# Attention decode on one core: the whole loads of values issued by ScalarE instead of SyncE

## The chip, the cores and the metric

The kernel runs on one core of a Trainium2 chip. A core has five instruction streams that run on their own and wait for each other by semaphores: TensorE (PE in the profile; its weight loads are PEld), VectorE (DVE), ScalarE (ACT), GpSimd (POOL) and SyncE (SP). Transfers between HBM and the on-chip memory are issued by an instruction on one of these streams and are then carried out by 16 DMA engines that the core's queues have in common. The metric is device time in microseconds: the median of several runs. Before the change it is 1301.58 us (three runs, 1301.52 to 1301.68).

## The reference

One token for each of B = 2 sequences is decoded through attention with a cache and then through a gated feed-forward block. D = 448, H = 16 heads of 256, 8192 cached positions, F = 1792, all in float32:

```
q = (layernorm(x) @ wq)                    # 2 x 16 heads x 256
p = softmax(q . k_cache / 16)              # 2 x 16 x 8192
o = p . v_cache                            # 2 x 16 x 256
h = x + o @ wo
n = layernorm(h)
out = h + ((n @ w_gate) * (n @ w_up)) @ w_down
```

Each of the 32 pairs of head and sequence has its own keys and its own values of 8192 x 256 floats, 8 MB each. So 512 MB of caches are read once, and next to them some 24 MB of weights. Nearly all of the work is reading.

## The kernel before

A pair of head and sequence is called a query here, numbered 0 to 31. Its keys lie in 128 partitions, 64 rows of 256 floats in each, so a whole load is 128 rows of 64 KB.

**Stages of a query i.** `load_k(i)` brings its keys. `scores(i, part)` multiplies them with q and sums over 256 on VectorE, first a part of 16 rows for each partition (4096 elements), then one of 48 (12288 elements). `top(i)` takes the maximum of each partition on VectorE; TensorE turns it over into `sm`. `softmax(i)` finishes the maximum (`nm`, VectorE), spreads it (TensorE, then `nb` on ScalarE), takes the exponentials into `p` (ScalarE) and sums them (TensorE); `norm(i)` takes the reciprocal `rl` on VectorE. `load_v(i)` brings the values. `mix(i)` multiplies `p` with them on TensorE into `o_ps`. `mixed(i)` copies the result out (`o_sb`, ScalarE), brings it into columns (TensorE into `sm`) and scales it by `rl` (`oT`, ScalarE); after every second query TensorE adds it through `wo` to `acc_ps`. After queries 1, 5, 9, ..., 25 `queries` computes the next q of two heads on TensorE, and ScalarE copies them into `q`.

**Buffers.** The keys have room for 112 of such rows in each partition (`k_sb`), one whole load and three quarters of another: the keys of query n+1 may be written when VectorE is done with the first part of query n. The values have room for one whole load (`v_sb`): the values of query n may be written when TensorE has mixed those of n-1.

**Order of the work.** The main loop over n (0 to 32) writes, on each engine, the work of several queries: scores of n, softmax of n-1 between the two steps of the first part, mix of n-1 at the end. In it the loads are written in this order: `load_v(n-1)` at its start, `load_k(n+1)` after the first part of the scores of n, and at n = 1, 9, 17, 25 a load of weights (`load_w`, 3.5 MB, the last one 2.6 MB). All of them are issued by SyncE, one after the other; each waits for its buffer there. The class `Orders` derives the waits from what each instruction reads and writes. Queries 0 to 27 (`i < LOOP`, with LOOP = EARLY = 28) are run by TensorE in a loop, and their loads of values count up one semaphore, `e_v`, that this loop takes. Values of queries 28 to 31 come in two or three pieces (the table `LATE`), some of them into room that the keys no longer need. Behind them come the weights of the feed-forward block, in the keys' room.

TensorE works in the order of the queries: for query i it turns the maximum over, spreads it, sums the exponentials, mixes, brings the result into columns and, where it is due, computes new q; only then does it turn over the maximum of query i+1. VectorE needs that last result (`nm`) between the two steps of the first part of query i+2.

```
        if n > 0:
            load_v(n - 1, parts[0])
        if n < NQ:
            scores(n, 0, (lambda: softmax(n - 1)) if n > 0 else None)
        ...
        if n + 1 < NQ:
            load_k(n + 1)
```

Of the kernel before, what the change touches and what calls it, by code (L numbers as in the profile page):

```python
# [68 lines left out]
LOOP = EARLY  # L69
# [146 lines left out]
def decode_block(nc, x, k_cache, v_cache, w, wg, wu, wd, out):  # L216
# [31 lines left out]
    buffers = {"k": k_sb, "v": v_sb}  # L248
# [17 lines left out]
    def keys(cache, i, lo, hi):  # L266
        h, b = divmod(i, B)
        return cache[b, h].rearrange("(p j) d -> p j d", p=P)[:, lo:hi, :]

    def load_keys(name, cache, i, lo, hi, buf, at, event=None):  # L270
        o.load(
            "SP", name, buffers[buf][:, at : at + hi - lo, :], keys(cache, i, lo, hi),
            writes=[(buf, at * DH, (at + hi - lo) * DH)], event=event,
        )

# [3 lines left out]
    def load_k(i, lo=0, hi=NJ):  # L279
        load_keys(f"d_k_{i}_{lo}", k_cache, i, lo, hi, "k", k_base(i) + lo)  # L280
# [8 lines left out]

    def load_v(i, part):  # L290
        lo, hi, buf, at = part
        load_keys(f"d_v_{i}_{lo}", v_cache, i, lo, hi, buf, at, "e_v" if i < LOOP else None)

    def load_w(name, k, lo, hi, event=None):
        o.load("SP", name, w_sb[:, lo:hi], w[k][:, lo:hi], writes=[("w", lo, hi)], event=event)
# [90 lines left out]
    def q_at(h):  # L386
        return h % 2 * (1 + h // 2 % 2)

    for k in range(2):
        for b in range(B):  # L390
            for c in range(DC):
                at = c * 2 * DH + (k * DH if c < DC - 1 else 0)
# [5 lines left out]
            at = q_at(k)  # L398
# [213 lines left out]
    for n in range(NQ + 1):  # L612
        hp, at = divmod(n, 2 * B)
        parts = v_parts(n - 1) if n > 0 else []
        if n > 0:
            load_v(n - 1, parts[0])
# [10 lines left out]
        for part in parts[1:]:  # L627
            load_v(n - 1, part)
# [37 lines left out]
    at = 0  # L666
# [191 lines left out]
```

## Time and profile before

| what | value |
|---|---|
| median of the runs | 1301.58 us (1301.52 to 1301.68) |
| span of the profiled execution, first to last instruction | 1300.5 us |
| VectorE busy | 1130.8 us (87%) |
| TensorE busy | 488.8 us (38%) |
| ScalarE busy | 62.6 us (5%) |
| read from HBM | 561.19 MB, 432 GB/s over the span |
| SyncE's queue, packets | 12096, 561.30 MB |
| ScalarE's queue, packets | 4 (the token's own 3.5 KB) |

Times in the views are in microseconds from the start of the span. In a timeline a row is a start, a duration, the engine, the line of the kernel and the operation as output<-input. Rows of SPq and ACTq are the instructions that issue a transfer on SyncE's and ScalarE's queue. All instructions are recorded by one helper, so that their line is L229 (L176 for transfers) and the names of the tiles tell them apart. In the chain of waits each row is a start, a duration and what the time went to; a row DMA begins with the issue of a transfer and ends with its landing.

### The profile page before, as it was taken

The numbers are of one execution on the slowest core, as the hardware profiler recorded it, in microseconds if no ns is written. First come the engines' busy times: TensorE is split into PE (matmuls) and PEld (weight loads), VectorE is DVE, ScalarE is ACT, GpSimd is POOL, SyncE is SP. The second block draws the span as 40 slices with busy tenths as digits, with TensorE's granted clock in tenths as the row PEclk, the third lists the DMA queues.
The fourth block names the chain that finished last, engine by engine and source line by source line (L and its number), as shares of the span: only waits on it lengthen the run. The fifth ranks groups of instructions, "written<-read, shape, count | busy, mean of one in ns | idle before, by whom it ended". The sixth has DMA issues, their size and how long they took to land.

```text
span 1300.5 us, 6955 instructions
## 1 busy us (share of the span) xinstructions
PE 488.8 (38%) x2972; PEld 168.9 (13%) x2972; DVE 1130.8 (87%) x275; ACT 62.6 (5%) x184; POOL 1.4 (0%) x9
## 2 busy tenths in 40 slices
PE   3035422363331633215343063432424334243368
PEld 2011100120100201002101021010111001010113
DVE  7996988888988689888889868898888897889991
ACT  1000000000000000000000000000000000000000
POOL 0000000000000000000000000000000000000000
PEclk8566756686656766558666576665766667666578
DMA  9999999999999999999999999999999999999998
GB/s 414 423 434 448 424 437 431 427 441 423 448 424 435 448 423 443 427 439 429 435 435 423 433 448 423 448 424 443 427 443 427 423 436 445 426 438 429 435 433 374
DMA packets 12111, 561.45 MB, mean 432 GB/s; under 512 B 1602, under 2 KB 1732, under 8 KB 1988
## 3 DMA queue, kind: packets, MB, share of 16 engines
q1 hardware_dynamic: 12096, 561.30, 99.8%
q8 instruction: 6, 0.10, 0.0%
q14 instruction: 5, 0.04, 0.0%
q10 hardware_dynamic: 4, 0.00, 0.0%
HBM read 561.19 MB, written 0.11 MB: 432 GB/s over the span
## 4 chain that ended last, share of the span: by engine, by line
DMA 70%; DVE 29%; PE 0%; issue 0%; SPq 0%
DMA k_sb<-in_A_k_cache_dram 68%; DVE k_sb L229 14%; DVE s L229 14%; DMA k_sb<-in_wd_dram 2%; DVE nm L229 0%; PE y_ps L229 0%; SPq L176 0%; DVE m L229 0%; PE sm L229 0%; DVE v_sb L229 0%; DVE rl L229 0%
## 5 line engine op out<-in xcount | busy, mean ns | idle before, releaser
L229 DVE TENSOR_TENSOR k_sb<-k_sb,q 128x12288 f32<-128x12288 f32 (+2 forms) x67 | 549.6, 8203 | 130.3 <-DMA k_sb<-in_A_k_cache_dram 130.3
L229 DVE TENSOR_REDUCE s<-k_sb 128x48 f32<-128x12288 f32 (+2 forms) x67 | 549.3, 8198 | 0.2
L229 PE MATMUL o_ps<-v_sb,p 128*2 128x512 f32 x2000 | 288.2, 739 | 397.7 <-PEq L183 387.6
L229 PEld LDWEIGHTS o_ps<-v_sb,p 128*2 128x2 f32 x2000 | 53.7, 97 | 603.8 <-issue 591.3
L229 PE MATMUL sm<-nm,ones 1*128 1x1 f32 x64 | 16.6, 326 | 191.7 <-PEq L183 175.1
L229 PE MATMUL sm<-ident,m 128*1 128x128 f32 x32 | 10.9, 341 | 137.0 <-PEq L183 106.1
L229 PE MATMUL q_ps<-w_sb,xb 128*128 128x256 f32 (+1 forms) x172 | 59.3, 503 | 0.0
L229 ACT ACTIVATE o_sb<-o_ps 128x512 f32<-128x512 f32 x32 | 19.1, 597 | 703.9 <-PE o_ps L229 703.9
L229 PE MATMUL sm<-sel,o_sb 128*128 128x1 f32 x256 | 33.7, 253 | 25.8 <-PEq L183 22.9
L229 PE MATMUL acc_ps<-w_sb,oT 128*2 128x448 f32 x60 | 36.6, 749 | 15.9 <-PEq L183 11.0
L229 PEld LDWEIGHTS sm<-nm,ones 1*128 1x128 f32 x64 | 14.6, 283 | 201.2 <-issue 183.5
L229 PEld LDWEIGHTS sm<-sel,o_sb 128*128 128x128 f32 x256 | 31.8, 195 | 55.6 <-issue 48.2
L229 PEld LDWEIGHTS q_ps<-w_sb,xb 128*128 128x128 f32 x172 | 33.7, 200 | 30.0 <-issue 27.6
L229 PE MATMUL sm<-lsum,ones 128*128 128x1 f32 x64 | 17.5, 342 | 26.0 <-PEq L183 23.1
L229 ACT ACTIVATE nb<-sm 128x1 f32<-128x1 f32 x32 | 5.5, 171 | 395.7 <-PE sm L229 395.7
L229 PEld LDWEIGHTS sm<-ident,m 128*1 128x1 f32 x32 | 2.6, 81 | 149.8 <-issue 115.3
L229 PEld LDWEIGHTS sm<-lsum,ones 128*128 128x128 f32 x64 | 15.6, 303 | 28.0 <-issue 24.7
L229 ACT ACTIVATE q<-q_ps,rstd 128x512 f32<-128x512 f32 (+1 forms) x18 | 11.5, 640 | 71.9 <-PE q_ps L229 71.9
L229 PE MATMUL o_ps<-k_sb,p 128*2 128x512 f32 x48 | 9.3, 934 | 6.1 <-DMA k_sb<-in_A_v_cache_dram 6.1
L229 ACT ACTIVATE p<-s,nb 128x64 f32<-128x64 f32 x32 | 11.1, 347 | 1.0
L229 DVE TENSOR_TENSOR v_sb<-k_sb,q 128x6144 f32<-128x6144 f32 x1 | 6.6, 6557 | 4.8 <-DMA k_sb<-in_A_k_cache_dram 4.8
L229 PE MATMUL q_ps<-k_sb,xr 128*32 128x256 f32 (+3 forms) x96 | 10.0, 506 | 1.6 <-DMA k_sb<-in_B_w_gate_dram 1.6
(79 smaller groups left out, 85.1 us busy)
## 6 DMA issues: line engine op xcount, KB each, us to landing
v_sb<-in_A_v_cache_dram SPq DMA_DIRECT2D x4, 4096.0 KB, 30.5
w_sb<-in_w_dram SPq DMA_DIRECT2D x3, 3584.0 KB, 37.8
v_sb<-in_A_v_cache_dram SPq DMA_DIRECT2D x1, 6144.0 KB, 24.3
k_sb<-in_A_k_cache_dram SPq DMA_DIRECT2D x1, 5120.0 KB, 24.6
v_sb<-in_A_v_cache_dram SPq DMA_DIRECT2D x2, 2048.0 KB, 27.3
k_sb<-in_A_v_cache_dram SPq DMA_DIRECT2D x1, 4096.0 KB, 35.3
k_sb<-in_B_w_gate_dram SPq DMA_DIRECT2D x1, 3136.0 KB, 32.4
k_sb<-in_A_k_cache_dram SPq DMA_DIRECT2D x1, 3072.0 KB, 11.6
```

Of the source, the lines that this page charges most:

```text
L229: o.put(engine, lambda: f(*args, **kw), r, w, mark, event)
```

## The change

The loads of values of queries 0 to 27 are issued by ScalarE instead of SyncE. Nothing else is changed: the same transfers into the same buffers, at the same place of the main loop, with the same semaphore.

```diff
-    def load_keys(name, cache, i, lo, hi, buf, at, event=None):
+    def load_keys(name, cache, i, lo, hi, buf, at, event=None, by="SP"):
         o.load(
-            "SP", name, buffers[buf][:, at : at + hi - lo, :], keys(cache, i, lo, hi),
+            by, name, buffers[buf][:, at : at + hi - lo, :], keys(cache, i, lo, hi),
             writes=[(buf, at * DH, (at + hi - lo) * DH)], event=event,
         )
...
-        load_keys(f"d_v_{i}_{lo}", v_cache, i, lo, hi, buf, at, "e_v" if i < LOOP else None)
+        load_keys(
+            f"d_v_{i}_{lo}", v_cache, i, lo, hi, buf, at, "e_v" if i < LOOP else None,
+            by="ACT" if i < LOOP else "SP",
+        )
```

On SyncE, around the first load of weights in the loop, the order before is:

```order
L176 DMA k_sb<-in_A_k_cache_dram 128x16384
L176 DMA v_sb<-in_A_v_cache_dram 128x16384
L176 DMA k_sb<-in_A_k_cache_dram 128x16384
L176 DMA w_sb<-in_w_dram 128x7168
L176 DMA v_sb<-in_A_v_cache_dram 128x16384
L176 DMA k_sb<-in_A_k_cache_dram 128x16384
L176 DMA v_sb<-in_A_v_cache_dram 128x16384
```

and after the change, from the first part of the first keys on:

```order
L176 DMA k_sb<-in_A_k_cache_dram 128x6144
L176 DMA k_sb<-in_A_k_cache_dram 128x10240
L176 DMA k_sb<-in_A_k_cache_dram 128x16384 x2
L176 DMA w_sb<-in_w_dram 128x7168
L176 DMA k_sb<-in_A_k_cache_dram 128x16384 x8
L176 DMA w_sb<-in_w_dram 128x7168
```

Keys and values no longer alternate there; eight loads of keys follow one another between two loads of weights.

On ScalarE, from the end of query 1 (the first query after which new q are computed) to the exponentials of query 3, the order before is:

```order
L229 ACTIVATE o_sb<-o_ps 128x512
L229 ACTIVATE oT<-sm,rl 128x2
L229 ACTIVATE q<-q_ps,rstd 128x2x256 x2
L229 ACTIVATE nb<-sm 128x1
L229 ACTIVATE p,lsum<-s,nb 128x64
L229 ACTIVATE o_sb<-o_ps 128x512
L229 ACTIVATE oT<-sm,rl 128x2
L229 ACTIVATE nb<-sm 128x1
L229 ACTIVATE p,lsum<-s,nb 128x64
```

and after the change:

```order
L229 ACTIVATE o_sb<-o_ps 128x512
L229 ACTIVATE oT<-sm,rl 128x2
L229 ACTIVATE q<-q_ps,rstd 128x2x256 x2
L176 DMA v_sb<-in_A_v_cache_dram 128x16384
L229 ACTIVATE nb<-sm 128x1
L229 ACTIVATE p,lsum<-s,nb 128x64
L229 ACTIVATE o_sb<-o_ps 128x512
L229 ACTIVATE oT<-sm,rl 128x2
L176 DMA v_sb<-in_A_v_cache_dram 128x16384
L229 ACTIVATE nb<-sm 128x1
L229 ACTIVATE p,lsum<-s,nb 128x64
```

The first of the two loads brings the values of query 2, the second those of query 3. A load now stands behind `oT` of the query before it and, after every fourth query, behind the two copies into `q` as well; on SyncE it waited for the end of the mix alone.

## The prediction

> **What bounds the kernel now.** I read the page first: its engines, the DMA slices and the queues.
>
> ```profile
> PE 488.8 (38%) x2972; PEld 168.9 (13%) x2972; DVE 1130.8 (87%) x275; ACT 62.6 (5%) x184; POOL 1.4 (0%) x9
> DMA  9999999999999999999999999999999999999998
> GB/s 414 423 434 448 424 437 431 427 441 423 448 424 435 448 423 443 427 439 429 435 435 423 433 448 423 448 424 443 427 443 427 423 436 445 426 438 429 435 433 374
> q1 hardware_dynamic: 12096, 561.30, 99.8%
> q10 hardware_dynamic: 4, 0.00, 0.0%
> ```
>
> No engine is full; the DMA engines are, in every slice but the last. A table of stretches (busy times, clock, DMA share, GB/s) says the same of single queries, and the chain of waits shows how a query's keys pass:
>
> ```profile
> 208.80:247.40 38.60, 12.12 (x77) 3.83 (x77) 35.01 (x7) 1.47 (x5) 0.00 (x0) 0.59 1.00 435
> 247.40:286.00 38.60, 18.20 (x95) 6.85 (x96) 35.01 (x7) 2.16 (x6) 0.00 (x0) 0.69 1.00 435
> 93.13 38.10 DMA k_sb<-in_A_k_cache_dram
> 140.22 29.89 DMA k_sb<-in_A_k_cache_dram
> 170.14 4.43 DVE k_sb L229
> 174.56 0.19 DVE nm L229
> 174.75 4.34 DVE s L229
> 179.11 29.67 DMA k_sb<-in_A_k_cache_dram
> 217.76 29.66 DMA k_sb<-in_A_k_cache_dram
> ```
>
> Keys are issued every 38.65 us (179.11 to 217.76); in that time one load of keys and one of values pass, so a load takes 19.33 us. A load of keys is on its way for 29.67 us: the first 10.3 it stands behind values. So SyncE's queue always holds 10 us of work when the next load joins it. VectorE, at 35.0 of 38.6 us, waits for keys. Only more bytes a second or fewer idle DMA moments could shorten this stage, and the DMA share is 1.00: what matters is whether the change keeps the engines fed.
>
> **The change, part by part.**
>
> *Issue.* 28 issues move. SyncE's cost 0.33 us; ScalarE's one issue before cost 0.53:
>
> ```profile
> 159.94 0.33 SPq L176 DMA_DIRECT2D v_sb<-in_A_v_cache_dram  x1
> 0.73 0.53 ACTq L176 DMA_DIRECT2D v_sb<-in_A_x_dram  x1
> 175.49 0.17 ACT L229 ACTIVATE nb<-sm 128x1 f32<-128x1 f32 x1 [13.48 <-PE sm L229]
> ```
>
> That is 15 us spread over an engine busy for 62.6; behind the load stands `nb`, which waits 13.48 us for TensorE anyway. I cost the issues at nothing; without that cover they would be 15 us.
>
> *When values are issued.* Timeline of an ordinary query (2) and of one with new q (5):
>
> ```profile
> 150.80 9.07 PE L229 MATMUL o_ps<-v_sb,p 128*2 128x512 f32 x64 [13.26 <-PEq L183]
> 161.75 0.26 ACT L229 ACTIVATE oT<-sm,rl 128x2 f32<-128x2 f32 x1 [1.21 <-PE sm L229]
> 266.87 9.06 PE L229 MATMUL o_ps<-v_sb,p 128*2 128x512 f32 x64 [12.73 <-PEq L183]
> 287.57 0.27 PE L229 MATMUL sm<-ident,m 128*1 128x128 f32 x1
> 287.77 0.69 ACT L229 ACTIVATE q<-q_ps,rstd 128x512 f32<-128x512 f32 x1 [2.75 <-PE q_ps L229]
> ```
>
> TensorE starts when values land. SyncE issued the next ones 9.1 us later (159.94). ScalarE must first finish `oT`, 11.2 us after landing (162.01), or in seven turns (after queries 1, 5, ..., 25) the second `q`, 21.6 us after (288.46).
>
> *Two queues instead of one.* Before, keys in flight kept the DMA busy while values were mixed, because loads passed in order of issue. With two queues nothing orders keys against values; q10's 4 packets show no sharing, so it is bounded from both sides: each engine finishes one load's share first (first rival), or the queues alternate. I take alternating: q1's 12096 packets are its 84 transfers times 144, 128 rows and 16 small ones each, so the unit an engine handles is a row of 64 KB, an eighth of its share, 2.42 us.
>
> *What alternating does.* Keys need 9.0 us from landing to next issue (170.12 to 179.11), values 11.2, so values fall back 2.2 us a query until two ties hold. First, both are then in flight together and land nearly together, and while both buffers are being used up nothing is in flight. Second, keys cannot run ahead: `nm` needs TensorE's turn of the maximum, which stands behind the previous query's mix and `oT`. From values landing: 11.2, about 0.5 to the turn, 0.3 for it, `nm` 0.2, reduction 4.34, 0.1 to the issue: keys are issued at 16.6, 5.4 us behind values.
>
> Start latency (issue to landing less own transfer time) is bounded by two issues into an idle DMA:
>
> ```profile
> w_sb<-in_w_dram SPq DMA_DIRECT2D x1, 896.0 KB, 4.8
> out_dram<-v_sb SPq DMA_DIRECT2D x1, 56.0 KB, 1.6
> ```
>
> 4.8 - 2.1 = 2.7 and 1.6 - 0.1 = 1.5; I take 2.0. Then, with even sharing: values have the DMA alone for 5.4 us; the other 13.93 take twice as long; they land 33.25 after their start, keys 5.4 later, and the next values start after 11.2 + 2.0: a query takes 46.45 us, 7.8 of them idle. A turn with new q takes 33.25 + 21.6 + 2.0 = 56.85. Keys by their own path would start at 38.65 + 9.0 + 2.0 = 49.65, before 46.45 + 5.4, so the tie holds, and it restores itself: keys further behind gain 2.2 us a query.
>
> *Start and end.*
>
> ```profile
> 26.07 0.33 SPq L176 DMA_DIRECT2D v_sb<-in_A_v_cache_dram  x1
> 56.95 12.94 DVE L229 TENSOR_TENSOR k_sb<-k_sb,q 128x12288 f32<-128x12288 f32 x1
> 57.05 0.33 SPq L176 DMA_DIRECT2D k_sb<-in_A_k_cache_dram  x1
> 64.97 9.31 PE L229 MATMUL o_ps<-v_sb,p 128*2 128x512 f32 x64 [10.20 <-PEq L183]
> 69.81 0.15 DVE L229 RECIPROCAL rl<-sm 128x1 f32<-128x1 f32 x1
> 1140.22 9.29 PE L229 MATMUL o_ps<-v_sb,p 128*2 128x512 f32 x64 [12.73 <-PEq L183]
> 1149.58 0.33 SPq L176 DMA_DIRECT2D v_sb<-in_A_v_cache_dram  x1
> 1159.42 4.43 DVE L229 TENSOR_TENSOR k_sb<-k_sb,q 128x4096 f32<-128x4096 f32 x1 [3.58 <-DMA k_sb<-in_A_k_cache_dram]
> 1296.47 2.03 PE L229 MATMUL y_ps<-k_sb,v_sb 128*32 128x112 f32 x64 [0.71 <-DMA k_sb<-in_wd_dram]
> ```
>
> Values 0 (issued 26.07) now share with keys 1, and what was through at 64.97 still is: both land there, keys about 2 us sooner, at 63. Keys 2 are issued 9.0 later, at 72 (57.05 before), and start at 74: 9 us idle. Values 1 wait for `oT` 0, whose `rl` (69.81) follows the long multiplication (56.95): issue 72 + 12.9 + 0.6 = 85.5, start 87.5. By halves (13.4 us of keys 2 done alone, then keys 2, the weights of 8.44 = 38.10 - 29.66, and keys 3 beside them) they land at 126.2 and values 2 start at 149.8. From there to the start of values 27 are 19 ordinary turns and 6 with new q: 882.6 + 341.1, so 1373.5; landing 1406.7; SyncE's first late values start at 1406.7 + 9.2 + 2.0 = 1417.9. From keys 29 landing (1159.4) to the last landing (1296.4) the DMA ran without a gap for 137.0 us, then 4.1 to the end. Sum: 1417.9 + 137.0 + 4.1 = 1559. The three other loads of weights fall into the idle 7.8 us and add at most 1 each.
>
> Row by row instead of evenly, values send three whole rows (7.25 us) before keys get a turn, and land at 7.25 + 5 x 4.83 = 31.4, 1.85 sooner; over 25 turns 46 us less: 1513. Rows are the unit, but sixteen engines need not turn in step and the slowest sets the landing; I take the middle, 1536, and add the 1.1 us by which the median of the runs exceeds the span: **1537 us**, 18% slower. Latency of 1.5 or 2.7 moves it by -13 or +18: own range 1490 to 1590.
>
> **Rivals.**
>
> *An engine finishes a load's share (eight rows) before it turns to the other queue.* The order is then that of before. A turn with new q leaves 21.6 + 2.0 - 19.33 = 4.3 us empty, unless weights (8.44) lie behind the keys, as in four of the seven; 3 x 4.3 = 13, so 1314 (1313 to 1317). Elsewhere the 10.3 us of work ahead cover the 2.1 us of delay. The same time follows if both queues feed one. For it: each engine's eight rows come from one instruction. Against it: rows are packets of their own in the counts. The Trainium skill, "DMA: Bandwidth & Descriptors", section "Queues, rings and completion order", says that a DMA engine goes round its queues packet by packet and that a packet is typically 9 to 17 descriptors; eight rows and an end would be one packet by that, and the time this rival's. No run shows yet which it is here.
>
> *Turns of several rows.* With four, values land after 12 rows, 29.0 us instead of 33.25: 25 x 4.25 = 106 less than 1559, 1453.
>
> *Not slower: order as in the first rival, and a second queue raises the rate,* one queue's rows filling the gaps between the other's. The 13 us are made up from 561.3 MB / (1293 - 14) = 439 GB/s on; at the slices' highest, 448, transfers take 1253 instead of 1293: 1314 - 40 = 1274. For it: slices of 448. Against: stretches cut at landings give 435 at a share of 1.00, so the 448 look like bytes booked at a row's end. With alternating rows no such rate could repay 235 us.
>
> **How the numbers follow.** Alternating 0.64, 1537; whole shares 0.20, 1314; coarse turns 0.07, 1453; not slower 0.09, of it 0.04 faster. About 0.2% (2.6 us) is what a measurement here can tell from no change; by it: faster 0.04, same 0.05, slower 0.91. The range takes in the second case and nearly all of the first: 1308 to 1595; the likeliest's own is 1490 to 1590.
>
> **What would show it.** Right: q10 with about 4036 packets and 235 MB; DMA slices at 8, some 365 GB/s; values and keys landing 33 to 39 us after issue, keys some 5 us behind; `nm` waiting for TensorE's `sm`; idle DMA after each landing, most after new q; VectorE busy as before but 74% of the span. Wrong: keys landing about 29.7 us after issue as now, which is the first rival, or a rate above 435 in stretches where both queues hold work. The forecast falls if queues do not alternate, and its size if keys are issued well before `oT`.

## The result, and the profile after

The changed kernel takes 1545.64 us (median of five runs, 1541.89 to 1546.97) against 1301.52 us (1301.33 to 1301.68) before: a ratio of 1.1871, 95% interval 1.1858 to 1.1883. The profiled execution spans 1544.3 us.

Lines of its page: engines, DMA slices, the two hardware queues and a group of instructions. The last two are from the list of transfers: how often keys and whole loads of values were issued, and the median us from issue to landing.

```profile
PE 480.4 (31%) x2972; PEld 164.2 (11%) x2972; DVE 1133.4 (73%) x275; ACT 62.6 (4%) x184; POOL 1.4 (0%) x9
DMA  9799889957899579886799958988589895988998
q1 hardware_dynamic: 8064, 326.42, 49.0%
q10 hardware_dynamic: 4036, 234.89, 36.1%
L229 DVE TENSOR_REDUCE nm<-sm 1x1 f32<-1x128 f32 x32 | 8.9, 278 | 123.3 <-PE sm L229 123.3
k_sb<-in_A_k_cache_dram SPq DMA_DIRECT2D x31, 34.0
v_sb<-in_A_v_cache_dram ACTq DMA_DIRECT2D x28, 34.0
```

The work is the same: VectorE is busy 1133.4 us (1130.8 before) and the two queues carry the same 561.3 MB, 234.89 of them now on ScalarE's. What changed is the time in which the DMA engines have nothing to do. The two queues' packets take 85.1% of the span, 1314 us; before it was 99.8%, 1298 us. So in the mean of the 16 engines 230 us of the span are empty, where 3 were. `nm` now waits 123.3 us for TensorE. Before, its line was:

```profile
L229 DVE TENSOR_REDUCE nm<-sm 1x1 f32<-1x128 f32 x32 | 8.7, 271 | 0.5 <-PE sm L229 0.5
```

One ordinary query in the timeline (values 7, keys 9):

```profile
379.46 0.26 ACT L229 ACTIVATE oT<-sm,rl 128x2 f32<-128x2 f32 x1 [1.21 <-PE sm L229]
379.46 0.33 ACTq L176 DMA_DIRECT2D v_sb<-in_A_v_cache_dram  x1
381.61 0.37 PE L229 MATMUL sm<-ident,m 128*1 128x128 f32 x1 [2.19 <-PEq L183]
382.02 0.28 DVE L229 TENSOR_REDUCE nm<-sm 1x1 f32<-1x128 f32 x1 [4.89 <-PE sm L229]
386.65 0.33 SPq L176 DMA_DIRECT2D k_sb<-in_A_k_cache_dram  x1
413.45 9.04 PE L229 MATMUL o_ps<-v_sb,p 128*2 128x512 f32 x64 [29.07 <-PEq L183]
420.59 4.42 DVE L229 TENSOR_TENSOR k_sb<-k_sb,q 128x4096 f32<-128x4096 f32 x1 [7.86 <-DMA k_sb<-in_A_k_cache_dram]
424.38 0.33 ACTq L176 DMA_DIRECT2D v_sb<-in_A_v_cache_dram  x1
```

Values are issued at 379.46. TensorE is then free to turn the maximum over (381.61), VectorE finishes it (382.02) and the first part of the scores, and the next keys are issued at 386.65, 7.2 us behind the values. Values land at 413.45, keys at 420.59. The next values are issued at 424.38: 44.9 us after the last, where a query took 38.65. Between 420.59 and 424.38 nothing is in flight, and a table of stretches cut at these points shows it in the last two columns (DMA share, GB/s):

```profile
413.50:420.60 7.10, 7.10 (x48) 1.35 (x52) 0.01 (x1) 0.00 (x0) 0.00 (x0) 0.72 0.68 295
420.60:424.40 3.80, 2.92 (x28) 1.26 (x20) 3.80 (x1) 0.62 (x2) 0.00 (x0) 1.00 0.00 0
424.40:432.30 7.90, 2.57 (x9) 0.93 (x9) 5.18 (x4) 0.85 (x4) 0.00 (x0) 0.93 1.00 398
432.30:458.40 26.10, 0.05 (x4) 0.08 (x8) 26.07 (x5) 0.00 (x0) 0.00 (x0) 0.50 1.02 442
```

The 0.68 of the first row is no idle time: a row of 64 KB counts whole in the stretch in which it starts, and two that start there give 2 x 2.42 / 7.10 = 0.68. By the packets recorded in the trace all 16 engines are at work until 419.5 us, none from 420.5 on, and the first row of the next values starts at 425.3. The same records show how the two queues share: in 15 of the 16 queries whose values are issued in an ordinary turn (no new q, no weights) the engines send four rows each of values alone, and then the other four in turns with rows of keys, one for one.

### The profile page after: what moved, and what is told of

Read it like the earlier page. It is cut to its first block, busy times and chain, and to the rows that moved or that the text cites. A ratio compares the mean times of both kernels' runs of the same rounds, so it can differ in the third digit from the quotient of the medians.

```text
span 1544.3 us, 6955 instructions
## 1 busy us (share of the span) xinstructions
PE 480.4 (31%) x2972; PEld 164.2 (11%) x2972; DVE 1133.4 (73%) x275; ACT 62.6 (4%) x184; POOL 1.4 (0%) x9
## 3 DMA queue, kind: packets, MB, share of 16 engines
q10 hardware_dynamic: 4036, 234.89, 36.1%
## 5 line engine op out<-in xcount | busy, mean ns | idle before, releaser
L229 PE MATMUL o_ps<-v_sb,p 128*2 128x512 f32 x2000 | 293.0, 748 | 828.2 <-PEq L183 808.4
L229 DVE TENSOR_REDUCE nm<-sm 1x1 f32<-1x128 f32 x32 | 8.9, 278 | 123.3 <-PE sm L229 123.3
L229 PE MATMUL acc_ps<-w_sb,oT 128*2 128x448 f32 x60 | 33.2, 687 | 15.9 <-PEq L183 11.0
L229 PE MATMUL sm<-lsum,ones 128*128 128x1 f32 x64 | 15.1, 306 | 26.1 <-PEq L183 23.1
## 6 DMA issues: line engine op xcount, KB each, us to landing
w_sb<-in_w_dram SPq DMA_DIRECT2D x3, 3584.0 KB, 46.1
```

The lines of the kernel that those rows point to most:

```text
L229: o.put(engine, lambda: f(*args, **kw), r, w, mark, event)
```

## The experiments

Theory 1 is that of the forecast: the queues take turns, keys and values then land close together, and the late issue by ScalarE together with the tie through `nm` leaves the DMA empty in every query. Rival A: the late issue alone does it. Rival B: using two queues alone does it, by a lower rate or otherwise.

### One queue, late issue

```diff
-        load_keys(f"d_v_{i}_{lo}", v_cache, i, lo, hi, buf, at, "e_v" if i < LOOP else None)
+        r = ()
+        if i < LOOP:
+            act(then, eps_t, AF.Copy, r=["eps_t"], w=["then"])
+            r = ["then"]
+        load_keys(
+            f"d_v_{i}_{lo}", v_cache, i, lo, hi, buf, at, "e_v" if i < LOOP else None, r
+        )
```

This is the kernel before with a small ScalarE instruction at the place of the moved load; SyncE waits for it. `r` is passed on as what the load reads.

> All loads stay on SyncE's queue, but each whole load of values waits there for a tiny ScalarE instruction that stands where the change put the load (behind oT and, after every fourth query, behind the two copies into q). So the issue is as late as in the changed kernel, with one queue. Theory 1 (queues take turns, and the lateness and the tie through nm then leave the DMA empty): with one queue a late load still finds the keys of 19.33 us ahead of it; only the seven turns with new q leave 21.6 + 2.0 - 19.33 = 4.3 us empty, here without weights to cover them, because these stand ahead of the values: 1301.5 + 30 = 1331 (1325 to 1337), values landing some 29 us after issue or less. Rival A (the late issue by ScalarE is the whole cause): near 1545. Rival B (the second queue itself is the cause, by a lower rate or by landing together whenever two queues are used): 1301 to 1331, no different from theory 1 here.

Measured: 1344.40 us, ratio 1.0319 (1.0301 to 1.0336), above the expected 1325 to 1337. Rival A falls: the same lateness costs 43 us with one queue, not 244. A turn with new q (values 6) shows where, and what a lone load costs:

```profile
274.12 1.89 PE L229 MATMUL o_ps<-v_sb,p 128*2 128x512 f32 x8 [12.79 <-PEq L183]
295.95 0.33 SPq L176 DMA_DIRECT2D v_sb<-in_A_v_cache_dram  x1
317.80 1.89 PE L229 MATMUL o_ps<-v_sb,p 128*2 128x512 f32 x8 [18.01 <-PEq L183]
```

Values 5 land at 274.12, values 6 are issued 21.8 us later and land 21.9 after that, with nothing ahead of them: 2.5 us more than the 19.33 of their transfer. Over the seven such turns the issue comes 20.9 to 24.8 us after landing (mean 23.1) and the lone load takes 21.8 to 22.2 (start latency 2.7): 7 x (23.1 + 2.7 - 19.33) = 45 us, the measured 43. The forecast of 1331 had 2.0 and 21.6 in the same formula.

### Two queues, early issue

```diff
         act(o_sb, o_ps[k], AF.Copy, r=[f"o_ps{k}"], w=["o_sb"], event=event("e_o", i))
+        if i + 1 < LOOP:
+            load_v(i + 1, v_parts(i + 1)[0])
...
-        if n > 0:
+        if n == 1 or n > LOOP:
             load_v(n - 1, parts[0])
```

> As the change, but ScalarE issues the values of query i+1 directly behind o_sb of query i, ahead of oT and q. Theory 1: values are issued 9.1 + 0.7 = 9.8 us after landing in every turn; keys stay tied at 16.6, in turns with new q at 25.6. After the first such turn keys are 15.8 us behind values, more than the 11 us (9.0 and a start of 2.0) in which their buffer is used up, so one of the two is always in flight; they lose 0.8 us a query and gain it back at the next turn with new q. Only the start (about 9 us empty, keys 1 and values 0 sharing) is left: 1308 to 1318. Rival A: no lateness, so 1301 to 1303. Rival B: two queues are as before, so 1500 or more.

Measured: 1372.38 us, ratio 1.0564 (1.0532 to 1.0595). Most of the loss is gone (173 of 244 us), so the second queue alone is not the cause either; but 71 us stay where theory 1 left 7 to 17. The timeline around keys 9 and values 8:

```profile
397.22 4.42 DVE L229 TENSOR_TENSOR k_sb<-k_sb,q 128x4096 f32<-128x4096 f32 x1 [5.43 <-DMA k_sb<-in_A_k_cache_dram]
406.19 0.33 SPq L176 DMA_DIRECT2D k_sb<-in_A_k_cache_dram  x1
406.95 9.86 PE L229 MATMUL o_ps<-v_sb,p 128*2 128x512 f32 x64 [3.03 <-PEq L183]
```

Keys land at 397.22, values 9.73 us behind them, and the next keys are issued at 406.19, too late to be at work when the values end: by the trace's packets all 16 engines are at work until 405.6 us, none at 406.8, and all again at 408.4. Each query takes 40.4 to 40.8 us (values land at 326.11, 366.49, 406.95), 1.9 over 38.65. By theory 1 values should fall back 0.8 us a query until the gap closes. They come back 9.3 us after landing in the mean (8.4 to 10.0) and keys after 9.0, which would still be 0.3 us a query; instead they stay 9.75 us behind, which is four rows of 64 KB (9.67). That led to the last experiment but two, with shorter rows.

### The queues the other way round

```diff
     def load_k(i, lo=0, hi=NJ):
-        load_keys(f"d_k_{i}_{lo}", k_cache, i, lo, hi, "k", k_base(i) + lo)
+        load_keys(
+            f"d_k_{i}_{lo}", k_cache, i, lo, hi, "k", k_base(i) + lo,
+            by="ACT" if 1 < i < LOOP + 2 else "SP",
+        )
```

Values stay on SyncE; `load_keys` takes `by` as in the change.

> Two queues the other way round: keys of queries 2 to 29 are issued by ScalarE, values, weights and the first and last keys by SyncE. Theory 1: values are issued 9.15 us after landing and keys 9.0, so neither falls back; the first keys and values pass in order on one queue, so that the phase of before, half a load apart, is kept. Nothing is empty except perhaps a few us where the keys return to SyncE: 1302 to 1309. Rival A: 1301 to 1309. Rival B (two queues in flight cost rate or fall together): 1450 or more.

Measured: 1314.91 us, ratio 1.0107 (1.0090 to 1.0124), a little over the expected 1302 to 1309 and far from rival B's 1450. Loads of both queues are in flight all through, and the same stretch of 200 us, here, in the kernel before, in the change and in the run with early issue, in this order, reads:

```profile
200.00:400.00 200.00, 78.35 (x463) 25.27 (x453) 181.75 (x36) 9.60 (x29) 0.00 (x0) 0.65 1.00 432
```

```profile
200.00:400.00 200.00, 71.81 (x418) 23.31 (x418) 180.22 (x37) 8.90 (x28) 0.00 (x0) 0.65 1.00 432
```

```profile
200.00:400.00 200.00, 61.36 (x336) 19.55 (x336) 145.48 (x31) 7.26 (x22) 0.00 (x0) 0.60 0.81 346
```

```profile
200.00:400.00 200.00, 74.55 (x415) 23.50 (x415) 172.15 (x34) 8.41 (x26) 0.00 (x0) 0.63 0.97 414
```

Two queues in flight move the 432 GB/s of one: no rate is lost and none is gained. Here, though, the rows pass almost load after load: from 308 to 323 us all 16 engines are at rows of keys, from 330 to 343 at rows of values. For rows in turns the change itself is the evidence: the median row of 64 KB takes 2.42 us in the turns there, on either queue, as it did before. The 13 us come at the four loads of weights, which now share SyncE's queue with the values: the first multiplication of a query's keys stands 6.8, 9.3, 11.7 and 13.0 us later than before after the first, second, third and fourth of them. Why each costs that, I did not test.

### Values in rows of 16 KB, keys in rows of 64 KB

```diff
+        for k in range(0, NJ, NJ // PIECES_V):
+            load_keys(f"d_v_{i}_{k}", v_cache, i, k, k + NJ // PIECES_V, buf, k, "e_v", by="ACT")
...
-            take("e_v", i, 16)
+            take("e_v", i, 16 * PIECES_V)
```

`PIECES_V` is 4; late values are loaded as in the change.

> As the change, but each whole load of values is four loads of 16 rows for each partition on ScalarE's queue, so that a row that an engine handles is 16 KB there and 64 KB on SyncE's. The mix still waits for all four. What is tested is how the queues take turns. If by whole rows: values get a fifth of the rate while keys are in flight; keys start 5.4 us behind and land 24.2 later, at 29.6 (26 us after issue), values at 38.65 (41 after issue), and a query takes 38.65 + 13.2 = 51.9 instead of 46.4: about 25 x 5.4 = 135 us over the changed kernel, near 1680. If by equal bytes: as the changed kernel, 1540 to 1560, both landing 33 to 34 us after issue. If an engine finishes a load's share first: values get a quarter load and then wait for a whole one of keys, slower than by whole rows.

Measured: 1733.29 us (one run). A query of it (values 5, keys 7):

```profile
311.77 1.84 ACTq L177 DMA_DIRECT2D v_sb<-in_A_v_cache_dram  x4
318.90 0.33 SPq L177 DMA_DIRECT2D k_sb<-in_A_k_cache_dram  x1
347.32 4.42 DVE L231 TENSOR_TENSOR k_sb<-k_sb,q 128x4096 f32<-128x4096 f32 x1 [2.33 <-DMA k_sb<-in_A_k_cache_dram]
352.96 1.88 PE L231 MATMUL o_ps<-v_sb,p 128*2 128x512 f32 x8 [36.33 <-PEq L185]
```

Keys, issued 7.1 us behind values, land 28.4 us after issue and 5.6 ahead of them; values take 41.2. Equal bytes (34 for both, 1540 to 1560 us) is refuted, and so is an engine that finishes a load's share first: keys would then land about 22 us after issue. Turns by whole rows, where values get a fifth, say 26 + 0.7 and 41, and fit. The total is 53 us over the expected 1680, which had left the rest at the change's price. Of these, 24 lie ahead of the landing of values 2 (196.3 us, in the change 172.7); the three turns with weights make up another part, with 58.5 to 60.6 us against 46.1 to 49.5 in the change.

### Both in rows of 16 KB

```diff
+        step = NJ // PIECES_V if 0 < i < LOOP + 2 else hi - lo
+        for k in range(lo, hi, step)[:: 1 if i % 2 or step == hi - lo else -1]:
+            load_keys(f"d_k_{i}_{k}", k_cache, i, k, k + step, "k", k_base(i) + k)
...
+        if part == 0 and 0 < i < LOOP + 2:
+            here = ("k", k_base(i) * DH, (k_base(i) + NJ) * DH)
```

The piece that has to wait for room goes first, and the first multiplication waits for all four, so that neither is earlier than before.

> As the change, but keys and values of queries 1 to 29 and 0 to 27 are all loaded in four pieces of 16 rows for each partition (the first multiplication still waits for all four pieces of its keys, the mix for all four of its values), so that the rows which take turns are 16 KB on both queues. Theory 1 with turns by whole rows: the turns come nearer to even sharing, where values land 33.25 us after their start instead of 31.4 for 64 KB rows; with a start latency of 2.7 (a lone load of values in the run with one queue and late issue landed 22.0 us after issue) even sharing gives 1559 + 0.7 x 25 = 1577 (1565 to 1590), against 1545 for the change. If the size of a row is not what sets the turns: 1540 to 1550.

Measured: 1542.10 us (1540.69 to 1543.18), ratio to the kernel before 1.1847 (1.1827 to 1.1867); the change's is 1.1871 (1.1858 to 1.1883). My expectation missed: the size of the rows makes no difference that can be told. A working from the timeline of the change above gives a reason: keys are issued not 5.4 but some 7 us behind values. Even sharing then lets values land 38.65 - 6.9 = 31.75 us after their start. By rows of 64 KB, as the packets show them, it is four rows alone, four in turns and one more row of keys ahead of the small end mark of the values: 9.67 + 19.34 + 2.42 = 31.4. The two nearly coincide.

### Early issue, both in rows of 16 KB

The edits of the last run and of the one with early issue together.

> As the run with two queues and early issue (1372), but with keys and values in pieces of 16 rows for each partition as in the run before. In that 1372 run values landed 9.75 us behind keys in every query, which is four rows of 64 KB (9.67), and keys came back into the DMA 11.7 us after landing: about 1.9 us empty in each query, although values should have fallen back 0.8 us a query and closed it. Theory 1a (the distance is held at a whole number of rows, because a start within a row's turn makes no difference): with rows of 16 KB the hold is gone, values drift to 11.7 us behind keys, and only the start and a few us at the weights are left: 1315 to 1335. Rival B' (two queues cost some 2 us a query by themselves, whatever the rows): 1372 as before.

Measured: 1331.22 us, ratio 1.0230 (1.0213 to 1.0247), within the expected 1315 to 1335 and 41 us under the same kernel with rows of 64 KB. In the 200 us from 200 to 400 the DMA share is back:

```profile
200.00:400.00 200.00, 73.23 (x437) 23.58 (x441) 178.75 (x36) 8.73 (x27) 0.00 (x0) 0.65 1.01 431
```

So two queues do not cost 2 us a query by themselves: rival B' falls. Theory 1a is not shown by this. The expected drift from 9.75 to 11.7 us did not take place: values land 21.8 us behind keys already at keys 2 (10.5 with rows of 64 KB), and 15 to 22 behind in the later queries (more at and just after the loads of weights, 12.8 in the last whole load). The two streams stood half a turn apart from the start, as in the kernel before, where it is 19.4; whether short rows would have let them leave 9.75 was not put to the test. Of the 30 us that remain, the start has less than half (keys 3 are first multiplied 12.6 us later than before, keys 10 14.8); the rest comes bit by bit over the later queries and their loads of weights (keys 28: 29.3).

### The turn of the maximum ahead of the mix

```diff
-        with common(i):
-            take("e_m", i)
+        with piece(i - 1, None if i == 0 else always if i == 1 else gone):
+            if i <= LOOP:
+                o.take("e_m")
             turn(mT_ps, m, r=["m"], w=["sm0"], mark="PE")
...
+        if 0 < n < NQ:
+            top(n)
         if n == NQ:
             mix(n - 1, parts[:-1])
...
-        if n < NQ:
-            if n == 0:
-                o.ops["PE"].append(lambda: turns())
+        if n == 0:
             top(n)
+            o.ops["PE"].append(lambda: turns())
```

> As the change, but TensorE turns over the maximum of query i+1 before it mixes query i, so that nm no longer waits for the end of the mix and oT: the tie of the keys to the values is moved by one query. Theory 1: keys may come back by their own path, 9.0 us after landing, while values need 11.2 (21.6 in turns with new q); values then fall behind until keys fill most of their gap; the seven turns with new q still leave 5 us or more, and now the mix waits for VectorE's maximum of the next query in some turns: 1380 to 1430. If the tie through nm plays no part and only the late issue and the two queues matter: 1530 to 1560.

Measured: 1417.47 us (one run), within the expected 1380 to 1430 and 128 us less than the change. The tie to TensorE's order is a part of the loss. It is moved, not removed: VectorE's longest waits are now those of `rl`, the reciprocal of the sum, which TensorE delivers behind the same mix.

```profile
DVE rl L229 <- PE sm L229: 162.3, 26, 16.1
DVE k_sb L229 <- DMA k_sb<-in_A_k_cache_dram: 89.4, 17, 17.1
```

### Issue ahead of the new q

```diff
         act(oT[:, :, b], oT_ps, AF.Copy, scale=rl_t[i % 2], r=["sm1", f"rl{i % 2}"],
             w=[("oT", b, b + 1)], event=event("e_oT", i))
+        if i + 1 < LOOP:
+            load_v(i + 1, v_parts(i + 1)[0])
```

The main loop leaves these loads out, as in the run with early issue.

> As the change, but ScalarE issues the values of query i+1 directly behind oT of query i, ahead of the two copies into q. Theory 1: values are issued 11.2 us after landing in every turn; keys tied at 16.6, in turns with new q at 25.6, so 14.4 us behind values there, losing 2.2 us a query until the next such turn: with 11.7 us for the keys' own gap, the empty time is 0, 0, 1.7 and 3.9 us in four queries, some 40 us in all, and 10 at the start: 1350; with distances held at whole rows as in the run with early issue up to 1400. If the seven late turns cost their 10.4 us each and no more: 1545 - 73 = 1472.

Measured: 1361.03 us (one run), between the expected 1350 and 1400, and 185 us less than the change by moving seven loads ahead of two copies of 0.69 us each and of what these wait for. A loss of the seven turns alone (1472) is refuted. What the seven late issues do is to bring values and keys together again each time: in the change the keys land 4.7 to 4.8 us behind the values after each of the last six of them. Here it is 14.3 us or more at these places, and over the next three queries the two come together again, to 4.7 to 11.9 us.

The four runs that vary queue and issue stand together like this (us over 1301.5):

| | prompt issue | issue behind `oT` and q |
|---|---|---|
| one queue | 0 (before) | 43 |
| two queues | 71 | 244 (the change) |

With short rows the 71 is 30. No version came out ahead of the kernel before; its DMA share was 1.00 already.

## Why the prediction was right

The forecast was 1537 us, own range 1490 to 1590; measured 1545.64.

**That the DMA is the bound.** Right: the same bytes, nearly the same rate while busy (561.3 MB in 1314 us, 427 GB/s, against 432), and 230 us empty.

**That the queues alternate, row by row.** Right, and the choice that decided: shown by the packets of the change, one row for one, and by the run with short rows of values, where keys got the larger share. The first rival, whole shares at 1314, is refuted by both, and with it the reading of a packet that I drew on there. The Trainium skill, "DMA: Bandwidth & Descriptors", section "Queues, rings and completion order", lets an engine go round its queues packet by packet; with a packet taken as one row of 64 KB or 16 KB, as the profile's counts of packets have it (4036 and 16132 on ScalarE's queue for the same 234.89 MB), the traces agree. A typical packet of 9 to 17 descriptors does not fit here: eight rows would have gone at one turn.

**That no second queue raises the rate.** Right: 432 GB/s with one queue and with two.

**The lateness.** Ordinary turns right, 11.2 us expected, 10.6 to 12.1 found from landing to the end of `oT`. Turns with new q were put at 21.6, from one row; to the end of the second copy they took 21 to 25.

**The tie through `nm`.** Right as a mechanism (123.3 us of waits), wrong in size: keys are issued 6.8 to 7.7 us behind the end of `oT` in 15 of 16 ordinary turns, not 5.4. Here the step "about 0.5 to the turn" failed: in the timeline above `oT` ends at 379.72 and TensorE's turn starts at 381.61, 1.9 us later; after every second query TensorE adds through `wo` first, and it is 2.8 (values 8: 424.64 to 427.42).

**The turns.** Ordinary ones take 45.0 us in the mean of 16 (46.45 evenly, 44.6 by rows expected), six with new q 58.7 (56.85), and the three with weights 49.5, 49.5 and 46.1, where I had added at most 1. From values 2 landing (172.70) to values 27 landing (1390.27) that is 1217.6 us, against 1223.7 evenly and 1200.7 with the 23 us taken off.

**The middle between even and row by row.** This step was wrong: with the tie as measured the two give nearly the same, in agreement with the run with all rows short, and taking 23 us off was not justified by anything that was there. The 16 ordinary turns came out 23 us shorter than evenly worked out all the same (16 x 1.45), which the later keys alone would give (values landing 31.75 instead of 33.25 us after their start). Values 2 landed at 172.7, 10.4 us earlier than worked out (the start was put too long), and the longer turns with new q and weights gave that back.

**Start and end.** Keys 2 were issued at 71.4 (72 expected), values 1 at 84.47 (85.5). From values 27 landing to the end: 154.0 us (152.3).

So the mechanism was right, and the agreement within 9 us (236 us forecast, 244 measured) is partly luck: the start came out 10.4 us under its term, the 25 turns 16.9 us over theirs (1217.6 against 1200.7) and the end 1.7 over, with opposite signs.

## What to carry to other kernels

A kernel that is bound by transfers and reuses each buffer needs something in flight while a buffer is being used up; one queue in which two streams alternate gives that for nothing, and two queues that share the engines give it only as long as the streams stay out of step. Before a stream is moved to another engine, look at what stands ahead of it there, and at which waits tie the two streams: a delay that a queue of waiting work hides is paid in full when it brings both streams to the same point. Rows of very different size on two queues share the engines by rows, not by bytes.

## What the runs showed of the hardware

Distances between landings come in whole rows. In the change keys land 4.7, 7.1 or 9.5 us behind values, near two, three and four rows of 2.42 us; values 6 and keys 8, for example:

```profile
368.00 8.29 PE L229 MATMUL o_ps<-v_sb,p 128*2 128x512 f32 x52 [34.76 <-PEq L183]
372.71 4.43 DVE L229 TENSOR_TENSOR k_sb<-k_sb,q 128x4096 f32<-128x4096 f32 x1 [10.71 <-DMA k_sb<-in_A_k_cache_dram]
```

A load's end mark, 16 packets of 4 B in the trace, takes a turn too: the last rows of values 7 end at 410.0 to 410.6 us, their marks stand at 412.4 to 413.0, behind one more row of keys. I had not expected that such steps can hold two streams at a distance which, by their own times, they should leave: with early issue it stayed at 9.75 us in most queries. How much of the 41 us between rows of 64 and of 16 KB that hold cost is open, because with the short rows the streams started further apart.

A new load starts later where the other queue is at work: in the change the first row starts 0.96 us after issue where nothing is in flight (values 7 and 8, for example), and 3.4 to 5.0 us after it where keys are issued while rows of values are at work.

In the run with one queue and late issue a load of 8 MB into an idle DMA took 21.8 to 22.2 us, 2.5 to 2.9 more than in a row of loads (19.33).
